# First unit's feed forward in float32 from weights right behind their bit operations, in a clustered attention with feed forward on one core

## The chip, the cores and the metric

The kernel runs on one core of one Trainium2 chip. The metric is the device time of one execution in microseconds (us). Before the change it is 861.57 us, the median of three runs (861.48 to 862.57).

## The reference

The reference is a clustered attention (4 batches, 8 heads, 768 positions, 64 numbers per head, 16 clusters per head) and a feed forward on its output. Every query and key is assigned to the nearest of its head's 16 centroids; a query attends only to keys of its own cluster.

```python
q_assign = np.argmax(np.einsum('bhsd,hcd->bhsc', q_n, c_n), axis=-1)
k_assign = np.argmax(np.einsum('bhsd,hcd->bhsc', k_n, c_n), axis=-1)
scores = np.where(q_assign == k_assign, scale * q @ k.T, -1e9)   # per batch and head
attn = softmax(scores)
x = (attn @ v) as 3072 tokens x 512
h = x @ w_in                                        # 512 x 2048
g = np.where(h >= 1, h, np.where(h <= -1, 0.0, (h + 1) ** 2 / 4))
out = (g @ w_out).astype(np.float32)                # 2048 x 512
```

The weights `w_in` and `w_out` reach the chip as float64; `q`, `k`, `v` are float32.

## The kernel before, in words

**Units and tiles.** The work is cut into 12 units, each a batch and a third of its queries (256 queries). A unit has four head pairs; each head pair has four attention tiles of 128 queries by 768 keys (`at_scores`, `at_soft`), and one product of probabilities and values with the row sums (`at_av`), which gives a quarter of the unit's `x`. A tile costs TensorE (PE) two to four matmuls into `pair`, VectorE (DVE) one custom operation that masks and takes the maximum (`sS<-pair,zero,er`), ScalarE (ACT) the exponential (`sS<-sS,sbi`), ACT a float16 copy (`hl<-sS`), GpSimd (POOL) the float16 rest (`hl<-sS,hl`), and the queue of SyncE (SP) a transposing DMA (`pT<-hl`). In unit 0 alone the tile stays float32 and PE transposes it (`pair<-idf,sS`); ACT copies it out (`pT<-pair`).

**Feed forward of a unit.** When the unit's `x` is there, it goes through 8 slices f of 256 hidden columns. `ffn1(u, f)` is 24 float16 matmuls 128x256: each operand is a sum of a float16 high and low half, and three of the four products are taken. Then DVE clamps (`r` from the bank), ACT squares, DVE multiplies and takes the maximum, ACT casts the high half of `g`, POOL subtracts for the low half. `ffn2(u, f)` is 12 float16 matmuls 128x512 that add into `pair`. `ffn_scale` makes a unit's powers of two and the clamps' bounds from the largest value of `x`'s source and of the weights, in short DVE operations.

**Weights.** 16 pieces (8 slices, `w_in` and `w_out`) arrive as float64 in `w`, `word` or two ends of other tiles. `w_bits` makes float32 of a piece: an ACT copy of the high words (`wk<-w`), a DVE shift (`wk<-wk`), PE sums of magnitudes (`<-wk,ones`) for a bound, and two DVE operations, which write in place (`w<-w,wk`, then `w<-w`; for the pieces in `word`, `word<-word,wk`, then `word<-word`). `w_sum` closes each slice's bound in short DVE operations (`w_am`, `w_iw`, `w_sw`). `w_split` then makes the float16 halves: an ACT scaling in place (`w<-w,w_sw`), an ACT cast (`w<-w`), a POOL subtraction (`w<-w`).

**What sets the order.** A recorder notes every operation with a step (`at(step, ...)`), plans all with rounds of forward and backward list scheduling from a table of costs (`BASE` rounds), then jiggles the priorities with a stored list of seeds (`NUDGES`), and issues each engine's instructions in the planned order, which is fixed at run time. Since one line issues all, every instruction of the profile of before stands at L351; groups are told apart by their names. A tile name's trailing number is its buffer. The steps around the change are `wat[i]` (bits of piece i), `sf` (feed forward), `PRO + 1` and `-7` (`v_bound` and `batch_scale` of batch 0, ahead of the first tile).

**Rings.** Temporary tiles rotate in rings: `wk` (two buffers), `word`, `r`, `g`, `x`. A tile can be written again once all that read it are done.

Of the kernel before, what the change touches and what calls it, by code (L numbers as in the profile page):

```python
# [474 lines left out]
def tile_clustered_attention_moe(  # L475
# [393 lines left out]
    def ffn_scale(us, fs):  # L869
# [4 lines left out]
        if n == GF:  # L874
            iw1, iw2, cs1 = (x[f0 // GF][:, :, a] for x, a in ((w_iw, 0), (w_iw, 1), (w_am, 0)))
        else:
            if not W:
                for i, (x, a) in enumerate(((w_iw, 0), (w_iw, 1), (w_am, 0))):
                    W[i] = const.tile([P, NF], F32, name=f"w_all{i}")
                    for g in range(NF // GF):  # L880
                        rec.gpsimd.tensor_copy(W[i][:, g * GF : (g + 1) * GF], x[g][:, :, a])
            iw1, iw2, cs1 = (W[i] for i in range(3))
# [129 lines left out]
    def at_av(b, hp, c):  # L1012
# [38 lines left out]
        xn = rs  # L1051
        if whole(b, c):
            rec.vector.scalar_tensor_tensor(
                out=xn, in0=pv, scalar=BX[b]["sv1"], in1=rs, op0=ALU.mult, op1=ALU.mult
            )
        else:
            rec.vector.tensor_tensor(out=xn, in0=pv, in1=rs, op=ALU.mult)
        if hp == 0:
            X[u] = new("x", [2, NP, CQ], F16)
        rec.scalar.copy(X[u][:, 0, hp], xn)  # L1060
        rec.gpsimd.tensor_tensor(out=X[u][:, 1, hp], in0=xn, in1=X[u][:, 0, hp], op=ALU.subtract)
# [285 lines left out]
```

## Time and profile before

| what | before |
|---|---|
| median of 3 runs | 861.57 us (861.48 to 862.57) |
| profiled execution, its own time | 860.33 us |
| span in its trace | 858.6 us |
| PE busy | 800.6 us (93%) |
| ACT busy | 664.1 us (77%) |
| DVE busy | 651.5 us (76%) |
| POOL busy | 546.6 us (64%) |
| DMA, mean rate over the span | 166 GB/s |

The trace is one execution. Its span runs from the first to the last recorded instruction; 1.73 us of the execution's time lie around it. "Busy" is the time in which at least one instruction of an engine was in flight. PE is the tensor engine's matmuls, PEld its loads of the stationary operand, which may lie beside matmuls. PEclk is the granted clock of the tensor engine as a share of full speed. A line of the timeline gives the start, the duration, the engine, the operation with the names of its tiles, and in brackets how long the engine had been idle and what released it. A float32 matmul appears in the trace as two records, a float16 one as one.

### The profile page before, as it was taken

The page shows a single profiled execution, that of the slowest core. Times are in us where ns is not written, and L with a number is a line of the kernel's source. Part 1 is how long each engine was busy: PE and PEld are TensorE (multiplying, and loading weights), DVE is VectorE, ACT ScalarE, POOL GpSimd, SP SyncE. Part 2 cuts the span into 40 slices and gives each one's busy share as a digit, 9 for nine tenths or more (in the row PEclk, how much of TensorE's full clock was granted, in tenths as well). Part 3 has the DMA queues.
Part 4 walks back from the last instruction along what each step waited for, and adds up shares of the span by engine and source line. Part 5 has one row for each costly group of instructions (what it writes and reads, how often), then busy time and mean ns, then how long its engine had stood idle before and what let it go on. Part 6 is the DMA issues. An engine that isn't in the chain of part 4 may idle for free.

```text
span 858.6 us, 19071 instructions
## 1 busy us (share of the span) xinstructions
PE 800.6 (93%) x7148; PEld 551.7 (64%) x7148; DVE 651.5 (76%) x1461; ACT 664.1 (77%) x1176; POOL 546.6 (64%) x527
## 2 busy tenths in 40 slices
PE   3666679999999999999999999999999999999998
PEld 3444456666676766767675766767676666676665
DVE  7999999988896877678887777668887767544322
ACT  6799999998777888778787788787788687776232
POOL 1146879887667777657666668757766667766222
PEclk9889989999999999999999999999999999999999
DMA  9896779789999989999999799999998778766100
GB/s 320 237 238 143 227 177 216 146 167 190 180 191 196 158 143 186 189 155 190 173 213 145 161 162 193 176 189 186 184 188 152 141 159 136 121 127 108 24 25 26
DMA packets 404766, 142.53 MB, mean 166 GB/s; under 512 B 372800, under 2 KB 396352, under 8 KB 404672
## 3 DMA queue, kind: packets, MB, share of 16 engines
q1 hardware_dynamic: 404672, 141.30, 82.1%
q8 instruction: 56, 0.92, 0.4%
q14 instruction: 38, 0.31, 0.1%
HBM read 40.40 MB, written 6.29 MB: 54 GB/s over the span
## 4 chain that ended last, share of the span: by engine, by line
PE 74%; DVE 15%; ACT 5%; issue 3%; DMA 2%; SPq 0%; POOL 0%; DVEq 0%; ACTq 0%
PE pair L351 37%; PE banka L351 10%; PE banki L351 9%; PE bankj L351 9%; PE bankh L351 9%; DVE sS L351 3%; DVE w L351 2%; ACT w L351 1%; ACT sS L351 1%; DMA kv<-in_k_dram 1%; DVE bankh L351 1%; DVE qn L351 1%; DVE r L351 1%; DVE wk L351 1%; DMA q<-qn 1%
## 5 line engine op out<-in xcount | busy, mean ns | idle before, releaser
L351 POOL TENSOR_TENSOR hl<-sS,hl 128x768 f16<-128x768 f32 x176 | 295.8, 1686 | 127.6 <-ACT hl L351 103.3
L351 PE MATMUL pair<-w,g 128*128 128x512 f16 x1152 | 271.2, 379 | 0.0
L351 PEld LDWEIGHTS <-w 128*128 128x128 f16 x2304 | 224.0, 98 | 48.3 <-issue 5.0
L351 DVE CUSTOM_DVE_ANT_0 sS<-pair,zero,er 128x768 f32<-128x768 f32 x192 | 193.9, 1011 | 50.9 <-PE pair L351 41.3
L351 ACT ACTIVATE sS<-sS,sbi 128x768 f32<-128x768 f32 x192 | 179.3, 934 | 60.0 <-DVE sbi L351 56.2
L351 PEld LDWEIGHTS <-g 128*128 128x128 f16 x1152 | 110.7, 98 | 114.3 <-issue 0.8
L351 PE MATMUL pair<-kv,q 128*128 128x384 f16 x768 | 159.9, 332 | 20.3 <-DVE sbi L351 8.7
L351 ACT CAST hl<-sS 128x768 f16<-128x768 f32 x176 | 143.7, 825 | 12.4 <-DMA pT<-hl 11.1
L351 POOL TENSOR_TENSOR g<-r,g 128x512 f16<-128x512 f32 x88 | 106.3, 1208 | 67.7 <-ACT g L351 56.1
L351 PEld LDWEIGHTS <-q 128*128 128x128 f16 x992 | 78.9, 99 | 76.9 <-issue 28.1
L351 PE MATMUL banka<-pT,kv 128*64 128x256 f16 (+1 forms) x1680 | 105.1, 279 | 0.2 <-DMA pT<-hl 0.2
L351 ACT ACTIVATE r<-r,f_ra,f_rs 128x512 f32<-128x512 f32 x88 | 71.3, 810 | 39.6 <-DVE r L351 39.4
L351 PEld LDWEIGHTS <-kv 128*64 128x64 f16 (+1 forms) x1824 | 92.7, 109 | 4.1 <-DMA kv<-n 0.9
L351 ACT CAST g<-r 128x512 f16<-128x512 f32 x88 | 53.7, 610 | 13.9 <-DVE r L351 9.4
L351 POOL TENSOR_TENSOR qn<-qn,phi 128x256 f16<-128x256 f16 x48 | 33.4, 715 | 30.9 <-DVE phi L351 21.4
L351 PE MATMUL bankh<-x,w 128*128 128x256 f16 x432 | 52.1, 273 | 0.7 <-DVE er L351 0.6
L351 PE MATMUL bankj<-x,w 128*128 128x256 f16 x408 | 50.1, 277 | 0.1
L351 POOL TENSOR_TENSOR w<-w 128x1024 f16<-128x1024 f32 x12 | 28.7, 2398 | 15.1 <-ACT w L351 15.0
L351 PE MATMUL banki<-x,w 128*128 128x256 f16 x312 | 37.6, 272 | 0.5 <-DVE r L351 0.5
L351 PE MATMUL banki<-wk,w 128*128 128x256 f16 x312 | 37.0, 272 | 0.0
L351 ACT ACTIVATE q<-q,phi 128x512 f16<-128x512 f16 x48 | 33.4, 715 | 4.3 <-DVE phi L351 2.7
L351 ACT ACTIVATION_READ_ACCUMULATOR sS<-sS,sbi 128x1 f32 x192 | 36.2, 189 | 0.0
(253 smaller groups left out, 1078.3 us busy)
## 6 DMA issues: line engine op xcount, KB each, us to landing
w<-in_moe_w_out_dram SPq DMA_DIRECT2D x14, 512.0 KB, 5.2
q<-in_q_dram SPq DMA_DIRECT2D x12, 512.0 KB, 4.9
kv<-in_k_dram SPq DMA_DIRECT2D x16, 384.0 KB, 4.2
kv<-in_v_dram SPq DMA_DIRECT2D x16, 384.0 KB, 4.2
out_dram<-o SPq DMA_DIRECT2D x11, 512.0 KB, 3.3
w<-in_moe_w_in_dram SPq DMA_DIRECT2D x10, 512.0 KB, 5.9
word<-in_moe_w_in_dram SPq DMA_DIRECT2D x6, 512.0 KB, 4.6
o<-in_v_dram SPq DMA_DIRECT2D x8, 384.0 KB, 4.1
```

Source lines behind the costliest of these rows:

```text
L351: fn(*args, **kw)
```

## The change

Unit 0's feed forward runs in float32. The last bit operation of a piece writes its float32 weights to `w32[a][f]`, the place in `wb` where the float16 halves later stand, and unit 0's matmuls read them there: 8 matmuls 128x256 for `ffn1` of a slice in place of 24, 4 matmuls 128x512 for `ffn2` in place of 12. Unit 0 has no `ffn_scale`, no cast and no subtraction for `g` and `x`; its `X[0]` is float32, written by DVE straight from the bank, and its clamp constants are fixed numbers. `w_split` comes later, after the slice's use by unit 0, and goes through a ring `ws` of three buffers (`wk[0]` and the two halves of `word`) back into `wb`. The bounds of the weights are closed by fours: `w_bound(g)`, two calls, each on 128x8, in place of one on 128x2 for each slice. The ring `w32` of the bit operations now has two buffers (`wk[0]` and `o`). `v_bound` and `batch_scale` of batch 0 stand at steps `VB + hp` and `VB + 5` in place of `PRO + 1` and -7. `WR`, the step from one piece's bits to the next, goes from 2.2 to 2.6; `BASE` from 40 to 29; `NUDGES` is another list with 147 entries in place of 201.

```diff
-BASE = 40
+BASE = 29
-    1600000002, 1600000012, 1600000016, 1600000020, 1600000031, 1600000035, 1600000041, 1600000076,
+    1700000013, 1700000016, 1700000028, 1700000032, 1700000035, 1700000049, 1700000073, 1700000096,
...
-    WA, WR = -4, 2.2
+    VB = 4
+    WA, WR = -4, 2.6
...
-    rings["w32"], rings["x"] = Ring(wk[:1]), Ring(tiles("x", 3, 4096) + wk + [word[:, :1024], word[:, 1024:]])
+    rings["w32"], rings["x"] = Ring(wk[:1] + rings["o"].bufs), Ring(tiles("x", 3, 4096) + wk + [word[:, :1024], word[:, 1024:]])
...
+        if hp == 0:
+            X[u] = new("x", [NP, CQ], F32) if u == 0 else new("x", [2, NP, CQ], F16)
         if whole(b, c):
             rec.vector.scalar_tensor_tensor(
-                out=xn, in0=pv, scalar=BX[b]["sv1"], in1=rs, op0=ALU.mult, op1=ALU.mult
+                out=X[u][:, hp], in0=pv, scalar=1 / UNIT, in1=rs, op0=ALU.mult, op1=ALU.mult
             )
+            return
...
+    w32 = [[wb[:, (2 * f + a) * 1024 : (2 * f + a + 1) * 1024] for f in range(NF)] for a in range(2)]
...
+    rings["ws"] = Ring([wk[0], word[:, :1024], word[:, 1024:]])
...
+        rec.vector.scalar_tensor_tensor(
+            out=dst, in0=hi, scalar=0x80000000, in1=to, op0=ALU.bitwise_and, op1=ALU.bitwise_or
+        )
...
+    def w_bound(g):
+        am, iw, sw = (x[:, g * GF : (g + 1) * GF].rearrange("p f a -> p (f a)") for x in (w_am, w_iw, w_sw))
+        mx = misc(2 * GF)
         rec.vector.tensor_scalar(
             out=mx, in0=am, scalar1=W_TINY, scalar2=2.0**-13 + 2.0**-19, op0=ALU.max, op1=ALU.mult
         )
         tiny_and(iw, mx, EXP_MASK2)
-        sw = new("w_sw", [2], F32, 4)
         rec.vector.reciprocal(sw, iw)
...
     def w_split(a, f):
-        t, tf = WL.pop((a, f))
-        tf = tf.bitcast(F32)
+        tf = new("ws", [1024], F32)
...
-        rec.scalar.activation(out=tf, in_=tf, func=AF.Copy, scale=sw)
+        rec.scalar.activation(out=tf, in_=w32[a][f].bitcast(F32), func=AF.Copy, scale=w_sw[:, f, a : a + 1])
...
+                for hp in range(NP if u == 0 else 0):
+                    rec.tensor.matmul(
+                        ph[:, s],
+                        w32[0][f].bitcast(F32)[:, hp * 256 + s * P : hp * 256 + (s + 1) * P],
+                        x[:, hp],
+                        start=(hp == 0),
+                        stop=(hp == NP - 1),
+                    )
...
+        if u == 0:
+            F[u, f] = r
+            return
...
-            at((b - 1) * SB + 22 + hp * 3 if b else PRO + 1, v_bound, b, hp)
-        at(b * SB - 13 if b else -7, batch_scale, b)
+            at((b - 1) * SB + 22 + hp * 3 if b else VB + hp, v_bound, b, hp)
+        at(b * SB - 13 if b else VB + 5, batch_scale, b)
...
+                if u == 0:
+                    sf = max(sf, wat[2 * f + 1] + 2)
+                    FS[u, f] = dict(io=1.0, lo=-1.0, hi=1.0, ra=half, rs=0.5, gs=1.0, first=f == 0, last=f == NF - 1)
+                    for x in range(2):
+                        at(max(sf + 3.5, wat[-1] + 1), w_split, x, f)
...
-        if a:
-            for x in range(2):
-                at(wat[i], w_split, x, f)
+        if a and f % GF == GF - 1:
+            at(wat[i] + 0.5, w_bound, f // GF)
```

The order on ACT, before, among unit 0's last tiles (`sS<-sS,sbi` is a tile's exponential, `pT<-pair` the copy of its transpose): the scaling `w<-w,w_sw` and the cast `w<-w` are a split.

```order
82 L351 ACTIVATE w_78<-w_78,w_sw_152 128x1024
83 L351 ACTIVATE sS_86,rs_163<-sS_86,sbi_156 128x768
84 L351 ACTIVATE sS_87,rs_163<-sS_87,sbi_157 128x768
85 L351 CAST w_78<-w_78 128x1024
86 L351 ACTIVATE pT_164<-pair_79 128x6x128
87 L351 CAST x_72<-rb_170 128x256
88 L351 ACTIVATE pT_164<-pair_80 128x6x128
89 L351 ACTIVATE q_66<-q_66,phi_149 128x512
90 L351 ACTIVATE wk_69<-w_78 128x1024
```

The order on ACT now, around the first split of the whole program, among tiles that follow unit 0's; `wk_69<-word_71` opens the bits of the last piece that arrives in `word`, `g_75<-g_75,half` is unit 0's square.

```order
129 L345 ACTIVATE wk_69<-word_71 128x1024
130 L345 ACTIVATE sS_85,rs_151<-sS_85,sbi_145 128x768
131 L345 CAST hl_167<-sS_86 128x768
132 L345 ACTIVATE g_75<-g_75,half 128x512
133 L345 ACTIVATE q_65<-q_65,phi_142 128x512
134 L345 CAST hl_168<-sS_87 128x768
135 L345 ACTIVATE wk_69<-w_78,w_sw 128x1024
136 L345 CAST w_78<-wk_69 128x1024
137 L345 ACTIVATE sS_86,rs_151<-sS_86,sbi_146 128x768
```

All 16 splits stand behind row 134 now; before, 12 of the 16 scalings stood ahead of row 134, the first of them at row 28.

The order on DVE, before, up to the fourth product of unit 0 (`rb<-banka,sv,rb`, the last quarter of its `x`):

```order
242 L351 RECIPROCAL f_hi_179<-f_inv_174 128x4
243 L351 RECIPROCAL f_lo_184<-banki 128x4
244 L351 TENSOR_SCALAR banki<-banki 128x4
245 L351 TENSOR_TENSOR f_gs_204<-banki,f_inv_174 128x4
246 L351 SCALAR_TENSOR_TENSOR w_78<-w_78 128x1024
247 L351 TENSOR_SCALAR f_ra_194<-banki 128x4
248 L351 SCALAR_TENSOR_TENSOR f_rs_199<-banki,f_inv_174 128x4
249 L351 SCALAR_TENSOR_TENSOR rb_170<-banka,sv_144,rb_170 128x256
```

The same place now; `x_72<-banka,rb_160` is the same product's last quarter.

```order
200 L345 SCALAR_TENSOR_TENSOR w_78<-word_71 128x1024
201 L345 ISA sS_85,sbi_145<-pair_80,zero,er_140 128x768
202 L345 ISA sbi_145 128x1
203 L345 TENSOR_REDUCE aq_125<-q_65 128x4
204 L345 RECIPROCAL w_sw<-w_iw 128x8
205 L345 TENSOR_REDUCE w_am<-bankh 128x2
206 L345 SCALAR_TENSOR_TENSOR x_72<-banka,rb_160 128x256
```

43 rows fewer stand ahead of this product: the short operations of `ffn_scale` and of the bounds, and some of the weights' bits.

More of the change, by code (lines that the diff above doesn't have):

```diff
@@ L655, in batch_scale @@
         e.update(isx=isx, sv=sv)
-        if b == 0:
-            e["sv1"] = const.tile([P, 1], F32, name="sv1")
-            rec.vector.tensor_scalar(out=e["sv1"], in0=sv, scalar1=1 / UNIT, scalar2=None, op0=ALU.mult)
     def transpose(out, nat, ps=None):
@@ L873, in ffn_scale @@
         f0, n = fs[0], len(fs)
[L874 to L882, printed above, removed]
+        iw1, iw2, cs1 = w_iw[:, :, 0], w_iw[:, :, 1], w_am[:, :, 0]
         def small(tag, cols=n):
@@ L1050, in at_av @@
         rec.scalar.copy(rs, rb)
-        xn = rs
+        if hp == 0:
+            X[u] = new("x", [NP, CQ], F32) if u == 0 else new("x", [2, NP, CQ], F16)
         if whole(b, c):
             rec.vector.scalar_tensor_tensor(
-                out=xn, in0=pv, scalar=BX[b]["sv1"], in1=rs, op0=ALU.mult, op1=ALU.mult
+                out=X[u][:, hp], in0=pv, scalar=1 / UNIT, in1=rs, op0=ALU.mult, op1=ALU.mult
             )
[L1056 to L1061, printed above, removed]
+            return
+        rec.vector.tensor_tensor(out=rs, in0=pv, in1=rs, op=ALU.mult)
+        rec.scalar.copy(X[u][:, 0, hp], rs)
+        rec.gpsimd.tensor_tensor(out=X[u][:, 1, hp], in0=rs, in1=X[u][:, 0, hp], op=ALU.subtract)
     X = {}
@@ L1067, in tile_clustered_attention_moe @@
     WL, WS = {}, {}
+    w32 = [[wb[:, (2 * f + a) * 1024 : (2 * f + a + 1) * 1024] for f in range(NF)] for a in range(2)]
     w1 = [view(wb[:, 2 * f * 1024 : (2 * f + 1) * 1024], [2, DM // P, 256], F16) for f in range(NF)]
     w2 = [view(wb[:, (2 * f + 1) * 1024 : (2 * f + 2) * 1024], [2, 2, DM], F16) for f in range(NF)]
-    w_am, w_iw = ([const.tile([P, GF, 2], F32, name=f"{x}{g}") for g in range(NF // GF)] for x in ("w_am", "w_iw"))
+    w_am, w_iw, w_sw = (const.tile([P, NF, 2], F32, name=x) for x in ("w_am", "w_iw", "w_sw"))
+    half = const.tile([P, 1], F32, name="half")
+    nc.gpsimd.memset(half, 0.5)
     WP = {}
     wd = 2 if w_wide else 1
+    rings["ws"] = Ring([wk[0], word[:, :1024], word[:, 1024:]])
     def w_load(a, f, part=None):
@@ L1102, in w_bits @@
         t = WL[a, f][0][:, (part or 0) * 512 :][:, :n]
+        dst = w32[a][f][:, (part or 0) * 512 :][:, :n]
         tf = t.bitcast(F32)
@@ L1106, in w_bits @@
             w_sum(a, f, part)
[L1107 to L1110 removed]
+            rec.vector.tensor_copy(dst, raw)
             return
@@ L1149, in w_sum @@
             return
-        am, iw = (x[f // GF][:, f % GF] for x in (w_am, w_iw))
-        mx = pc[:, 2, :2]
-        rec.vector.tensor_reduce(out=am, in_=pc[:, :2], op=ALU.max, axis=AX.X)
+        rec.vector.tensor_reduce(out=w_am[:, f], in_=pc[:, :2], op=ALU.max, axis=AX.X)
+    def w_bound(g):
+        am, iw, sw = (x[:, g * GF : (g + 1) * GF].rearrange("p f a -> p (f a)") for x in (w_am, w_iw, w_sw))
+        mx = misc(2 * GF)
         rec.vector.tensor_scalar(
@@ L1180, in ffn1 @@
             with rec.group():
-                for hp in range(NP):
+                for hp in range(NP if u == 0 else 0):
[6 more added lines that the diff above has]
+                    )
+                for hp in range(0 if u == 0 else NP):
                     for i, (wa, xa) in enumerate(((0, 0), (0, 1), (1, 0))):
@@ L1190, in ffn1 @@
         phf = ph.rearrange("p s q -> p (s q)")
-        r = new("hl" if u == NU - 1 else "r", [2 * CQ], F32, 1)
+        r = new("g" if u == 0 else "hl" if u == NU - 1 else "r", [2 * CQ], F32, 1)
         rec.vector.tensor_scalar(out=r, in0=phf, scalar1=e["lo"], scalar2=e["hi"], op0=ALU.max, op1=ALU.min)
@@ L1209, in ffn2 @@
         po = F[u]
+        if u == 0:
+            with rec.group():
+                for s in range(2):
+                    for t in range(CT):
+                        rec.tensor.matmul(
+                            po[t],
+                            g[:, s * CQ + t * P : s * CQ + (t + 1) * P],
+                            w32[1][f].bitcast(F32)[:, s * DM : (s + 1) * DM],
+                            start=(f == 0 and s == 0),
+                            stop=(f == NF - 1 and s == 1),
+                        )
         terms = [(s, i, *x) for s in range(2) for i, x in enumerate(((0, 0), (0, 1), (1, 0)))]
@@ L1213, in ffn2 @@
         parts = [(terms, [t]) for t in range(CT)] if end else [(terms[:3], range(CT)), (terms[3:], range(CT))]
-        for part, ts in parts:
+        for part, ts in parts if u else ():
             with rec.group():
@@ L1303, in tile_clustered_attention_moe @@
             at(wat[i], w_bits, a, f, p)
-        if a:
-            for x in range(2):
-                at(wat[i], w_split, x, f)
+        if a and f % GF == GF - 1:
+            at(wat[i] + 0.5, w_bound, f // GF)
     rec.step = -99
```

25 lines of the change are left out of this document (4 added, 21 removed), and 44 rows, old and new, of the table NUDGES.

## The prediction

> **What bounds the kernel now.** I read the page's slices first, then busy time by stage, then the chain of events around the first feed forward. In the slices each digit is a fortieth of the span:
>
> ```profile
> span 858.6 us, 19071 instructions
> PE 800.6 (93%) x7148; PEld 551.7 (64%) x7148; DVE 651.5 (76%) x1461; ACT 664.1 (77%) x1176; POOL 546.6 (64%) x527
> PE   3666679999999999999999999999999999999998
> ```
>
> PE has nines from about the sixth slice to the end and is loose only before. The windows put numbers on that (columns: stretch, its length, then PE, PEld, DVE, ACT, POOL busy, granted clock, DMA share, GB/s):
>
> ```profile
> 0.00:111.00 111.00, 65.98 (x643) 45.40 (x644) 104.01 (x255) 95.86 (x148) 49.05 (x66) 0.92 0.83 232
> 111.00:236.70 125.70, 119.57 (x1072) 82.14 (x1071) 112.54 (x257) 112.59 (x201) 100.29 (x85) 0.99 0.89 179
> 236.70:400.00 163.30, 163.17 (x1498) 113.94 (x1495) 129.85 (x284) 129.10 (x242) 113.60 (x110) 1.00 0.97 177
> 400.00:800.00 400.00, 397.39 (x3553) 274.33 (x3552) 288.07 (x644) 309.36 (x563) 271.48 (x257) 1.00 0.86 161
> ```
>
> Up to 111 us PE is idle for 45 us while DVE is busy for 104 of 111: DVE paces the start. From 111 to 236.7 PE idles 6.1 us; after it 2.7 us in 563. So a change ahead of 236.7 passes to the end one for one if PE's remaining work stays the same, and what happens there must be followed to one event. I take unit 1's last `ffn1` (M), since it needs the last weights' halves:
>
> ```profile
> 233.77 2.75 PE L351 MATMUL pair<-w,g 128*128 128x512 f16 x12
> 236.36 0.46 PE L351 MATMUL bankh<-cT,kv 128*128 128x32 f16 x12
> 236.66 2.78 PE L351 MATMUL bankj<-x,w 128*128 128x256 f16 x24
> 239.28 0.81 PE L351 MATMUL pair<-kv,q 128*128 128x384 f16 x4
> ```
>
> M is at 236.66. Start to next start also gives two prices: 24 float16 matmuls 128x256 take 2.62 us (109 ns each), 12 of 128x512 take 2.59 us (216 ns). The first feed forward starts so:
>
> ```profile
> 105.74 2.59 DVE L351 SCALAR_TENSOR_TENSOR w<-w 128x1024 uint32<-128x1024 uint32 x1
> 108.40 0.47 DVE L351 SCALAR_TENSOR_TENSOR rb<-banka,sv,rb 128x256 f32<-128x256 f32 x1
> 109.48 0.40 ACT L351 CAST x<-rb 128x256 f16<-128x256 f32 x1
> 109.95 0.98 POOL L351 TENSOR_TENSOR x<-rb,x 128x256 f16<-128x256 f32 x1 [2.70 <-ACT x L351]
> 110.98 3.04 POOL L351 TENSOR_TENSOR w<-w 128x1024 f16<-128x1024 f32 x1
> 111.09 1.27 PE L351 MATMUL bankj<-x,w 128*128 128x256 f16 x5
> ```
>
> DVE comes to the last quarter of `x` at 108.40, then ACT and POOL add 2.2 us before PE starts at 111.09.
>
> **The first feed forward starts earlier.** The order puts 43 fewer DVE rows ahead of that product: four bit operations, two shifts, one tile, one maximum of V, and some 30 short rows. The rows that price them (instructions by form between 18 and 109 us, then two of the timeline):
>
> ```profile
> L351 DVE SCALAR_TENSOR_TENSOR w<-w 128x1024 uint32<-128x1024 uint32 x10 | 14.1, 1412 | 0.0
> L351 DVE SCALAR_TENSOR_TENSOR w<-w,wk 128x1024 uint32<-128x1024 uint32 x11 | 13.4, 1220 | 0.0
> L351 DVE TENSOR_SCALAR wk<-wk 128x1024 uint32<-128x1024 uint32 x12 | 9.1, 759 | 0.5 <-ACT wk L351 0.5
> 109.72 0.68 DVE L351 TENSOR_SCALAR wk<-wk 128x1024 uint32<-128x1024 uint32 x1
> 11.49 2.67 DVE L351 TENSOR_REDUCE v_am<-kv 128x1 bf16<-128x768 f32 x3
> 14.08 0.41 DVE L351 TENSOR_REDUCE mx<-bankh 128x16 f32<-128x256 f32 x1
> ```
>
> Successive DVE instructions overlap by about 0.08 us, so 4×1.15 + 2×0.61 + 0.93 (a tile) + 0.85 (a maximum) + some 30 short ones at 0.13 = 11.6 us less. Next, the bit operations run slower where POOL subtracts: `w<-w` took 1.41 on average and 2.59 at 105.74, the shift 0.76 against 0.68. With no split ahead, 10×0.19 + 12×0.08 and the longest single excess go, about 4.5 us together (bounds 2 to 5.5). Against it, `v_bound` leaves the start, where its 2.67 us stood in DVE's wait for the first labels (the maximum at 14.08): DVE now idles there, 2.5 us (bounds 0 to 2.7). So the last quarter ends at 108.87 − 11.6 − 4.5 + 2.5 = 95.3, and with no cast or subtraction behind it PE starts at about 95.5, 15.6 us earlier. ACT and PE can follow: ACT loses 12 splits from that stretch.
>
> **Unit 0's matmuls cost more.** No matmul of this shape in float32 is in the trace; the nearest is unit 0's product with V, against its float16 form:
>
> ```profile
> 56.65 2.76 PE L351 MATMUL banka<-pT,kv 128*64 128x256 f32 x24
> 240.27 2.13 PE L351 MATMUL banka<-pT,kv 128*64 128x256 f16 x36
> L351 PEld LDWEIGHTS pair<-idf,sS 128*128 128x128 f32 x96 | 11.8, 156 | 13.6 <-ACT sS L351 13.2 <-issue 0.4
> L351 PEld LDWEIGHTS <-w 128*128 128x128 f16 x277 | 27.5, 100 | 6.8 <-issue 1.0
> ```
>
> The 24 float32 records are 12 matmuls, in pairs: 460 ns a pair against 118, so 3.9 times, and I take 4. A slice costs 8×4×0.109 + 4×4×0.216 = 6.95 us in place of 5.21: 1.74×8 = 13.9 us more on PE. The load of float32 weights took 156 ns against 100. I take it as hidden, since the float32 product with V stayed at the rate of its passes; bounds 0 to 11 us (rival below). The Trainium skill, "TensorE: Matmul & The Clock Gate", section "Weight-path perf modes — Fast Weight Load (FWL) and DoubleRow", says that the fast load is on for 128 weights whose type is not FP32, which speaks against the change; the two rows agree in direction, and by it nothing is lost while a load is shorter than the matmul ahead of it.
>
> **PE alone.** From PE's start to M, before has 114.3 us of PE work in 125.6 us. To it come the 13.9 us; 2.9 us of tiles that used to stand ahead of the start; and 1.6 us that now stands ahead of M instead of behind it: 132.7 us. With 6 to 11 us of idle time and half clock (before lost 11.3), M by PE alone would be 95.5 + 132.7 + 6 to 11 = 234.2 to 239.2, at best guess 235.5.
>
> **The splits stand later, and ACT must do them all.** This is the step on which I choose. The ring of the splits starts with `wk[0]`, which is free when DVE has done the first bit operation of the third piece staged in `word`:
>
> ```profile
> 145.50 1.52 DVE L351 SCALAR_TENSOR_TENSOR word<-word,wk 128x1024 uint32<-128x1024 uint32 x1
> ```
>
> In before it ends at 147.02. DVE's work ahead of it is about the same in the order of after (0.4 us more), so it comes at 147.0 − 5.5 (POOL's hindrance up to there) + 2.5 + 0.4 = 144.4 (bounds 142 to 147). The order then has 127 ACT instructions from the first split's scaling to the cast of slice 7's `w_in`. Their prices (ACT by form, 60 to 170 us):
>
> ```profile
> L351 ACT ACTIVATE sS<-sS,sbi 128x768 f32<-128x768 f32 x26 | 24.4, 940 | 1.5 <-DVE sbi L351 1.3
> L351 ACT CAST hl<-sS 128x768 f16<-128x768 f32 x16 | 13.0, 824 | 0.0
> L351 ACT CAST w<-w 128x1024 f16<-128x1024 f32 x9 | 10.3, 1147 | 0.0
> L351 ACT ACTIVATE w<-w,w_sw 128x1024 f32<-128x1024 f32 x8 | 10.1, 1257 | 1.7 <-DVE w L351 1.7
> L351 ACT ACTIVATE r<-r,f_ra,f_rs 128x512 f32<-128x512 f32 x7 | 5.7, 808 | 0.0
> L351 ACT CAST g<-r 128x512 f16<-128x512 f32 x6 | 3.7, 611 | 1.3 <-DVE rs L351 1.3
> L351 ACT ACTIVATE qn<-q,sq 128x256 f16<-128x256 f32 x8 | 3.8, 514 | 0.0
> ```
>
> Neighbours overlap by about 0.1 us, except that an exponential's read of its sum follows it (0.93 in all). 21 exponentials are 19.5, 22 casts `hl` 16.1, 15 scalings 17.1, 15 casts of weights 15.5, 10 squares 7.2, 7 casts `g` 3.6, together 79.0; 37 shorter ones at 0.41 (the `qn` row) are 15. So ACT needs 94 us without a gap, and POOL's subtraction follows:
>
> ```profile
> L351 POOL TENSOR_TENSOR w<-w 128x1024 f16<-128x1024 f32 x12 | 28.7, 2398 | 15.1 <-ACT w L351 15.0
> ```
>
> M = 144.4 + 94 + 2.4 = 240.8, 5.3 us behind PE alone and 4.1 us later than before. ACT was busy for 112.6 of 125.7 us in that window of before; now it has slack ahead of 144 and none behind. After M, PE has 1.6 us less to do. The bounds of M are 142 + 92 + 2.4 = 236.4 and 147 + 95 + 2.4 + 1.6 (PE's tiles and ACT waiting for each other) = 246.
>
> **Small edits.** The bounds by fours and the fixed constants are in the DVE count; they save POOL four copies. Behind M the order differs through the new list. The last stretch:
>
> ```profile
> 800.00:858.60 58.60, 54.48 (x392) 35.89 (x390) 17.00 (x23) 17.20 (x26) 12.21 (x11) 0.99 0.05 19
> ```
>
> PE idles 2.7 us from M to 800 and 4.1 here, so I price the new list at nothing, bounds −2 to +2.
>
> **The sum.** Against the profiled execution (858.6 + 1.73 = 860.33) the change is +4.1 − 1.6 = +2.5. The median lies 1.24 us higher, so 861.57 + 2.5 = 864.1, rounded to 864.0. Its own range, with the bounds of M, is 859.7 to 869.3, the ends only if every bound falls to one side.
>
> **The rivals.**
>
> *PE alone sets M* (faster). If the splits keep ahead of unit 1, because DVE frees `wk[0]` earlier or ACT runs denser, M is 235.5 and the time 861.57 − 1.1 − 1.6 = 858.9. For it: PE was the engine without idle time from 111 us on. Against it: the last 94 us of ACT work begin only at 144. It decides if the first split starts before about 139.
>
> *Both nearly meet* (no difference). The splits come a little earlier or denser, or the start comes at 98 in place of 95.5: M at about 238, time 861.3. This also covers the case that the change does not do what it says, the first feed forward held back by another wait than DVE's.
>
> *POOL sets M* (slower). From the first split to slice 7's subtraction POOL has 22 subtractions `hl`, 15 of weights, 7 of `g`, 6 of `x` and 15 short ones:
>
> ```profile
> L351 POOL TENSOR_TENSOR hl<-sS,hl 128x768 f16<-128x768 f32 x34 | 58.0, 1711 | 13.9 <-ACT hl L351 12.4 <-DVE sbi L351 1.1
> L351 POOL TENSOR_TENSOR g<-r,g 128x512 f16<-128x512 f32 x14 | 17.4, 1243 | 10.8 <-ACT g L351 10.8
> L351 POOL TENSOR_TENSOR x<-rb,x 128x256 f16<-128x256 f32 x11 | 8.6, 783 | 2.7 <-ACT x L351 2.7
> ```
>
> That is 37.6 + 36.0 + 8.7 + 4.7 + 8 = 95 us, from 146.6 (the first cast's end): 241.6, level with ACT. The means hold some stretched rows already. If half the subtractions of weights take the 3.04 us of the one at 110.98, beside DVE, that is 7.5×0.64 = 4.8 more, M = 246.4, and the time 861.57 + 9.7 − 1.6 = 869.7. The Trainium skill, "SBUF — State Buffer", states that DVE and GpSimd lock a shared port pair and that the loser blocks for a whole instruction; the 2.59 us at 105.74 agrees, and by it the splits' move shifts that loss from the start to the stretch before M.
>
> *Float32 loads in the open* (slower). 8×12 = 96 matmuls, two records each: 192×(156 − 100) = 10.8 us on PE's path: M = 246.3, so 869.6. Against it: the float32 rows above.
>
> **How the numbers follow.** About 0.2%, 1.72 us, is what a measurement of this kernel can tell from no change: faster is below 859.85, slower above 863.29. The forecast (ACT) has 0.39, of which 0.05 falls within 0.2%; PE alone 0.25; both nearly meeting 0.23; POOL 0.08; loads 0.05. So faster 0.25, same 0.28, slower 0.39 − 0.05 + 0.08 + 0.05 = 0.47. The range takes PE alone's lower end (234.2: 857.6) as 857.5 and goes up to 869.0, nearly the forecast's upper end; POOL's case, the loads and the tails are left out.
>
> **What would show it.** Right: the first `ffn1` at 94 to 98 with float32 records; the first split's scaling on ACT at 142 to 147; ACT without a gap from there; M at 240 to 242, with PE's idle time between 200 and 240 ended by POOL `w` or ACT `w`. Wrong: PE without gaps before M and M at 235 (PE alone); POOL dense and ACT waiting for it (POOL); float32 `ffn1` of 8 matmuls over 4.2 us (loads); a first `ffn1` after 100, which undoes the first term.

## The result, and the profile after

The changed kernel takes 855.91 us (median of 6 runs, 855.04 to 856.83), the kernel before 862.0 us beside it (6 runs, 859.35 to 862.72). The ratio is 0.9934, with a 95% interval of 0.992 to 0.9949: faster by 0.66%, where 864.0 was forecast. The time lies below the range. The profiled span went from 858.6 to 854.1 us.

The page of the changed kernel, busy time and PE's slices (each a fortieth of the span):

```profile
span 854.1 us, 18789 instructions
PE 808.4 (95%) x7052; PEld 557.1 (65%) x7052; DVE 641.5 (75%) x1408; ACT 653.2 (76%) x1158; POOL 530.1 (62%) x510
PE   3676999998999999999999999999999999999997
```

PE's nines begin at the fifth slice instead of the seventh. The windows, cut at the first feed forward (91.9), the first split (141.4) and M, unit 1's eighth first product (234.66):

```profile
0.00:91.90 91.90, 60.50 (x619) 42.28 (x620) 83.41 (x209) 69.00 (x115) 18.77 (x47) 0.93 0.89 256
141.40:234.66 93.26, 88.01 (x738) 59.71 (x736) 80.08 (x171) 89.88 (x148) 87.98 (x62) 1.00 0.87 172
234.66:400.00 165.34, 162.99 (x1462) 112.70 (x1459) 125.86 (x285) 132.71 (x248) 118.89 (x113) 1.00 0.90 171
400.00:800.00 400.00, 400.00 (x3603) 277.03 (x3601) 288.70 (x643) 310.17 (x566) 267.64 (x259) 1.00 0.85 159
```

Ahead of the first feed forward POOL is busy for 18.8 us in place of 49.1, ACT for 69.0 in place of 95.9. That work now stands between 141 and 235 us, where ACT (89.9 of 93.3) and POOL (88.0) are nearly full. The first feed forward, on DVE and then PE:

```profile
91.64 0.41 DVE L345 SCALAR_TENSOR_TENSOR x<-banka,rb 128x256 f32<-128x256 f32 x1
91.91 1.89 PE L345 MATMUL banki<-x,w 128*128 128x256 f32 x8
94.29 1.89 PE L345 MATMUL banki<-x,w 128*128 128x256 f32 x8
96.02 1.89 PE L345 MATMUL bankh<-x,w 128*128 128x256 f32 x8
```

The last quarter of `x` ends at 92.05, against 108.87, and PE starts 19.2 us earlier than before (it may take the first three head pairs while the last quarter is made). M, with PE's rows around it:

```profile
232.28 2.13 PE L345 MATMUL banka<-pT,kv 128*64 128x256 f16 x36
234.34 0.47 PE L345 MATMUL bankh<-cT,kv 128*128 128x32 f16 x12
234.66 2.78 PE L345 MATMUL bankj<-x,w 128*128 128x256 f16 x24
```

M came 2.0 us earlier (236.66 before), and from M to the end it takes 619.4 us in place of 621.9. Together that is the span's 4.5 us. Up to M, PE has some 10 us more work (185.5 us before, 195.7 now, by its windows) and waits 12 us less.

### The profile page after: what moved, and what is told of

Its sections match the earlier page's. It is cut to its first block, busy times and chain, and to the rows that moved or that the text cites. A ratio compares the mean times of both kernels' runs of the same rounds, so it can differ in the third digit from the quotient of the medians.

```text
span 854.1 us, 18789 instructions
## 1 busy us (share of the span) xinstructions
PE 808.4 (95%) x7052; PEld 557.1 (65%) x7052; DVE 641.5 (75%) x1408; ACT 653.2 (76%) x1158; POOL 530.1 (62%) x510
## 4 chain that ended last, share of the span: by engine, by line
PE 69%; DVE 1%; ACT 0%; issue 0%; DVEq 0%
PE pair L345 34%; PE banka L345 10%; PE bankh L345 9%; PE banki L345 9%; PE bankj L345 7%; DVE sS L345 0%; DVE bankh L345 0%; ACT hl L345 0%; DVE qn L345 0%; ACT qn L345 0%; DVE n L345 0%; ACT r L345 0%; DVE mx L345 0%; DVE o L345 0%; ACT o L345 0%
## 5 line engine op out<-in xcount | busy, mean ns | idle before, releaser
L345 PE MATMUL pair<-w,g 128*128 128x512 f16 (+1 forms) x1120 | 277.0, 391 | 0.5 <-ACT o L345 0.5
L345 PEld LDWEIGHTS <-w 128*128 128x128 f16 x2112 | 204.6, 98 | 43.8 <-issue 5.6
L345 PEld LDWEIGHTS <-g 128*128 128x128 f16 x1056 | 101.0, 98 | 106.1 <-issue 1.9
L345 POOL TENSOR_TENSOR g<-r,g 128x512 f16<-128x512 f32 x80 | 94.0, 1176 | 56.8 <-ACT g L345 53.9
L345 ACT ACTIVATE r<-r,f_ra,f_rs 128x512 f32<-128x512 f32 x80 | 64.7, 809 | 31.7 <-DVE r L345 31.5
L345 PE MATMUL bankj<-x,w 128*128 128x256 f16 (+1 forms) x424 | 58.2, 289 | 4.3 <-DVE r L345 1.6
L345 ACT CAST g<-r 128x512 f16<-128x512 f32 x80 | 48.9, 611 | 14.4 <-DVE r L345 8.5
L345 PE MATMUL bankh<-x,w 128*128 128x256 f16 (+1 forms) x376 | 46.5, 277 | 0.0
L345 PE MATMUL banki<-x,w 128*128 128x256 f16 (+1 forms) x288 | 40.5, 291 | 0.4 <-DVE w_iw L345 0.4
L345 POOL CAST rr<-rs 128x4 f16<-128x4 f32 x48 | 15.8, 328 | 36.6 <-DVE bankj L345 21.0
```

The costliest lines, as they stand in the source:

```text
L345: fn(*args, **kw)
```

## The experiments

All edits but the two of the list keep the planned order of the kernel that they start from: the planner sees the unchanged costs, and the edit is made when the instructions are issued. vb_early and split2_early then move the few operations that they name. A table first; "start" is PE's first matmul of the feed forward (in late4 it takes three head pairs at 93.1 and has the last quarter of `x` only after 97.2), "split" the first split's scaling, all from the one profiled execution of each. "Ratio" is to the kernel before, run beside it, with its interval.

| kernel | edit | us | ratio | start | split | M |
|---|---|---|---|---|---|---|
| before | – | 862.0 | 1 | 111.1 | – | 236.7 |
| after | – | 855.91 | 0.9934 (0.992–0.9949) | 91.9 | 141.4 | 234.7 |
| before_list0 | no list of seeds | 870.29 | 1.0107 (1.0092–1.0122) | 114.5 | – | 242.3 |
| after_list0 | no list of seeds | 857.5 | 0.9963 (0.995–0.9976) | 92.4 | 140.0 | 236.6 |
| cast2 | after, 16 split casts twice | 867.59 | 1.0077 (1.0061–1.0092) | 93.2 | 142.4 | 246.6 |
| cast2_six | after, 6 split casts twice | 860.22 | 0.999 (0.9981–0.9999) | 91.3 | 140.9 | 238.5 |
| scale_less | after, 6 scalings short | 854.57 | 0.993 (0.9908–0.9951) | 91.9 | 141.2 | 233.4 |
| ffn1_half | after, 13.9 us less PE, unit 0 | 856.46 | 0.9953 (0.9939–0.9967) | 93.2 | 140.8 | 234.0 |
| u1_cut | after, 10.7 us less PE, unit 1 | 854.87 | 0.9928 (0.9902–0.9953) | 93.2 | 142.4 | 234.6 |
| both_less | scale_less and u1_cut | 856.06 | 0.9943 (0.9925–0.9961) | 91.9 | 141.5 | 235.9 |
| late4 | after, 4.5 us more DVE at 91 us | 861.2 | 1.0 (0.999–1.001) | 93.1 | 146.6 | 239.8 |
| dve_less | after, 4.6 us less DVE | 855.59 | 0.9936 (0.9921–0.9951) | 92.0 | 141.0 | 234.2 |
| vb_early | after, V's maxima early | 855.53 | 0.9938 (0.9923–0.9953) | 93.6 | 142.4 | 235.6 |
| relu_u0 | after, clamp from DVE to ACT | 857.69 | 0.9957 (0.9941–0.9974) | 92.5 | 143.6 | 236.4 |
| split2_early | after, two splits early | 856.14 | 0.9945 (0.993–0.996) | 93.3 | – | 235.4 |
| before_pool2 | before, split subtractions twice | 892.62 | 1.0367 (1.0349–1.0384) | 127.5 | – | 266.4 |
| before_memset | before, memset for subtraction | 862.6 | 1.0026 (1.0014–1.0039) | 110.8 | – | 238.8 |
| before_scale | before, scalings short | 863.97 | 1.0021 (1.0011–1.0032) | 114.1 | – | 241.2 |
| before_scale_memset | both | 862.82 | 1.0021 (1.0008–1.0035) | 111.3 | – | 239.3 |

Kernels that are the same up to 90 us start their feed forward at 91.3 to 93.3 us (the last section shows that the granted clock goes with this), so a difference of one or two microseconds between single profiles is no finding; the medians and the distance from the split to M carry the argument.

**Is it the list?**

```diff
-NUDGES = (
-    1700000013, 1700000016, 1700000028, 1700000032, 1700000035, 1700000049, 1700000073, 1700000096,
...
+NUDGES = ()
```

> The changed kernel with an empty list of seeds, so that only the planner's rounds set the order. Theory (the float32 feed forward makes the gain, by an early start of unit 0's feed forward on PE): the first feed forward still starts near 92 us, against 111 in the kernel before, and the time stays below that of the kernel before without its list by 3 to 9 us; by itself it is 857 to 866. Rival (the new list makes the gain): the two kernels without lists take the same time within 2 us, both above 862.

> The kernel before with an empty list of seeds. Theory: 863 to 870, with the first feed forward at 109 to 114 us, and 3 to 9 us above the changed kernel without its list. Rival (the list makes the gain): within 2 us of the changed kernel without its list.

The rival falls. Without lists the change is worth more: 0.9963 / 1.0107 = 0.986, about 12 us. The old list takes 9 us off the kernel before, the new one some 2.5 us off the changed one (0.9963 against 0.9934). Each kernel kept its own number of planner's rounds, 40 and 29. The early start is there without a list, the first matmuls of the feed forward in after_list0 and in before_list0:

```profile
92.44 1.89 PE L324 MATMUL banki<-x,w 128*128 128x256 f32 x8
```

```profile
114.46 1.91 PE L324 MATMUL bankj<-x,w 128*128 128x256 f16 x8
```

**Does ACT set M, or PE?** First more work on ACT:

```diff
         rec.scalar.copy(whi, tf)
+        rec.nodes[-1].times = 2
...
-                for fn, args, kw in x.calls:
-                    fn(*args, **kw)
+                for i, (fn, args, kw) in enumerate(x.calls * x.times):
+                    if i not in x.drop:
+                        fn(*args, **kw)
```

> The changed kernel in its own order, with each split's ACT cast issued twice: 16 casts of 1.04 us more on ACT, 14 of them (14.6 us) up to slice 7's w_in half. Theory (PE alone sets M, the halves are ready 6.5 us before): slice 7's w_in subtraction ends at 228.2 + 14.6 = 242.8, M waits for it, 234.7 + 8.1 = 242.8, and the time is 855.9 + 8.1 = 864. Rival (ACT already sets the end): 855.9 + 14.6 = 870.5. Rival (ACT is nowhere near): 856.

> The changed kernel in its own order, with the ACT cast of the splits of slices 1, 2 and 3 issued twice: 6 x 1.04 = 6.2 us more on ACT ahead of M. New theory (ACT sets the pace, 3.4 us idle): M and the time 3 to 6 us later, 859 to 862. Rival (PE sets M and the halves are 6.5 us early): 856.

From the split to M it took 93.3 us in the changed kernel, 104.2 in cast2 and 97.6 in cast2_six: 10.9 us for 14.6 us of casts, 4.3 for 6.2. This does not fit the theory that PE alone sets M until the halves come (864, 856): extra ACT work costs about 0.7 us for each microsecond from the first on. Then less work on PE, in unit 0 and in unit 1:

```diff
                         stop=(hp == NP - 1),
                     )
+                    rec.open.drop = (1, 2)
```

> The changed kernel in its own order, leaving out two of four head pairs in unit 0's first product: 32 float32 matmuls 128x256 fewer, 32 x 0.433 = 13.9 us of PE work. Theory (PE work sets M until the halves do, 6.5 us on): M goes to 228.3 and the time to 855.9 - 6.4 = 849.5. Rival (only PE's work counts): 855.9 - 13.9 = 842.0. Rival (the splits already set M): no change, 856.

```diff
+                    rec.open.drop = (1, 2, 4, 5, 7, 8, 10) if u == 1 else ()
                     for i, (wa, xa) in enumerate(((0, 0), (0, 1), (1, 0))):
```

> The changed kernel in its own order, leaving out 14 of 24 matmuls in each slice of unit 1's first product: 1.53 us a slice, 10.7 us of PE work less between 170 and M. New theory (from the first split at 141 to M, ACT sets the pace with at most 3.4 us of idle time, PE waits on it through the tiles): M comes 1 to 3 us earlier, the time is 853 to 855. Rival (PE's work sets M): M comes 6.5 us earlier, when the halves are ready, and the time is 849.4 or less.

ffn1_half settles what the float32 work of unit 0's first product costs. Its windows up to the end of unit 0's last `ffn1` and from there to M (unit 0's last three `ffn2`, in float32 too, lie in the second), then the same two of the changed kernel:

```profile
93.20:160.00 66.80, 54.44 (x368) 34.76 (x367) 63.52 (x109) 54.91 (x94) 46.97 (x35) 1.00 0.93 193
160.00:234.00 74.00, 68.30 (x610) 45.45 (x610) 63.43 (x144) 71.26 (x118) 68.75 (x50) 1.00 0.89 173
```

```profile
91.90:161.50 69.60, 66.85 (x432) 46.87 (x431) 65.95 (x112) 56.00 (x95) 46.16 (x35) 1.00 0.88 188
161.50:234.66 73.16, 68.32 (x611) 45.45 (x610) 62.54 (x142) 70.39 (x117) 67.88 (x50) 1.00 0.87 173
```

PE has 12.4 us less to do in the first stretch, and the split and M stand where they stood: PE just waits longer (12.4 us idle in place of 2.8), and the time is not shorter. Unit 0's extra passes lie beside work of DVE. In u1_cut nearly the same holds behind 161 us: 9.2 us less PE work shortens the stretch by 1.1 us. What PE saves there it mostly waits for DVE's `sbi`, that is for a tile's scores to be read out of `pair`: 7.8 us in 8 waits, against 1.3 in 2 in the changed kernel (window, then PE's row of waits in u1_cut and in the changed kernel):

```profile
162.50:234.60 72.10, 59.11 (x513) 35.83 (x513) 64.44 (x142) 70.28 (x117) 67.93 (x50) 1.00 0.91 177
```

```profile
PE pair L346 <- DVE sbi L346: 7.8, 8, 1.9
```

```profile
PE pair L345 <- DVE sbi L345: 1.3, 2, 0.9
```

Then less work on ACT, and on both:

```diff
+        if f in (4, 5, 6):
+            rec.nodes[-1].calls[0][2].update(out=tf[:, :64], in_=w32[a][f].bitcast(F32)[:, :64])
```

> The changed kernel in its own order, with the ACT scaling of the splits of slices 4, 5 and 6 on 64 of 1024 columns (the rest of these halves is left out): 6 x 1.05 = 6.3 us less ACT work between unit 0's end and M. Theory (ACT, busy for 70.4 of 73.2 us there, sets that stretch, with POOL and PE 5 us behind): M 3 to 5 us earlier, the time 851 to 853. Rival (PE sets it): 856.

> The edit of scale_less and that of u1_cut together (14 of 24 matmuls of unit 1's first product left out): ACT 6.3 and PE 10.7 us less before M. Theory (three engines are within 5 us of each other there, and POOL is left with 67.9 of 73.2 us): M 4 to 6 us earlier, 850 to 852, hardly more than by scale_less alone. Rival (PE and ACT limit in turns): 846 to 849.

```profile
161.20:233.40 72.20, 68.16 (x612) 45.46 (x611) 61.90 (x142) 66.64 (x118) 68.18 (x50) 1.00 0.86 175
```

```profile
161.50:235.90 74.40, 60.45 (x512) 36.30 (x511) 65.88 (x143) 66.53 (x118) 66.94 (x50) 0.98 0.89 171
```

Here the theory that ACT alone sets the stretch falls too. With 3.8 us less ACT work (first line, scale_less) it is 1.0 us shorter, and with PE and ACT both relieved (second line, both_less) it is not shorter at all. This profile is the slowest of both_less's five executions, but its median, 856.06, is no shorter either. So work added on ACT between the first split and M costs most of its length, while work taken from ACT, from PE or from both behind 161 us gives 1 us or nothing. PE, ACT and POOL are each busy for 68 to 70 of 73 us there, DVE for 62.5, and a tile goes from PE through DVE, ACT, POOL and a DMA back to PE; what holds the stretch once two of them are relieved stays open.

**Does DVE set the start and unit 0's feed forward?**

```diff
             apply_absolute_value=True,
         )
+        rec.nodes[-1].times = 5 if u == 2 else 1
```

> The changed kernel in its own order, with the maximum over Q of unit 2 (DVE, 1.13 us start to start), which stands just ahead of the last quarter of unit 0's x, issued five times: 4.5 us of DVE work more at 90 us. New theory (DVE's bit operations on the weights pace unit 0's feed forward from its start to about 158 us, and 14 us of float32 work are hidden in PE's waiting there): everything on DVE comes 4.5 us later, unit 0's last float32 matmul at 166, the first split at 146, M at 239, the time 860.4. Rival (PE's work from its start on sets M, as the prediction's rival had it, less the 7.6 us of idle time): 856 to 858.

```diff
             out=dst, in0=hi, scalar=0x80000000, in1=to, op0=ALU.bitwise_and, op1=ALU.bitwise_or
         )
+        if f < 2:
+            rec.nodes[-1].gone = True
+            rec.nodes[-2].calls[0][2]["out"] = dst
```

> The changed kernel in its own order, leaving out the last bit operation (the sign) of the four pieces of slices 0 and 1: 4 x 1.14 = 4.6 us less DVE work ahead of the first feed forward. Theory (DVE's work paces the start and up to 141 us, one for one): start at 87 to 89, the first split at 137, the time 851.5. Rival (other waits lie close behind DVE at the start, as with V's maxima moved): 854 to 856.

Again one direction only. In late4 the five maxima take 6.23 us at 90.69, the last quarter of `x` follows at 97.23, the split at 146.6, and the time is 861.2, 5.3 us more:

```profile
90.69 6.23 DVE L346 TENSOR_REDUCE aq<-q 128x4 bf16<-128x1024 f32 x5
96.83 0.19 DVE L346 RECIPROCAL w_sw<-w_iw 128x8 f32<-128x8 f32 x1
96.94 0.37 DVE L346 TENSOR_REDUCE w_am<-bankh 128x2 f32<-128x256 f32 x1
97.23 0.41 DVE L346 SCALAR_TENSOR_TENSOR x<-banka,rb 128x256 f32<-128x256 f32 x1
```

In dve_less 4.6 us less DVE work leaves the start at 92.0. (The granted clock from 60 to 92 us was 0.89 there and 1.00 in the changed kernel; by the last section that may hide about a microsecond.) DVE waits for PE instead, 2.0 us for tiles (`sS`) and 4.3 us ahead of maxima (`mx`), against 0.4 and 2.4 in the changed kernel. DVE's waits up to 93 us, dve_less and then the changed kernel (in all, times, longest):

```profile
DVE mx L345 <- PE bankj L345: 3.0, 2, 2.4
...
DVE sS L345 <- PE pair L345: 2.0, 4, 0.7
DVE mx L345 <- PE bankh L345: 1.3, 1, 1.3
```

```profile
DVE mx L345 <- PE bankj L345: 2.4, 1, 2.4
...
DVE sS L345 <- PE pair L345: 0.4, 1, 0.4
```

Two more edits in this direction were meant to be faster than the changed kernel:

```diff
+        early("v load", "weights")
+        early("v bound", "labels")
```

> The changed kernel with V's loads of batch 0 issued ahead of the weights' first loads and three maxima of V (0.87 us each) put into DVE's 2.4 us wait for the first labels, all else in its own order. Theory (DVE paces): DVE is about 2.2 us earlier from there on, and the time is 853.7. Rival (no DVE time at the start reaches the end, or the weights' loads come later by as much): 855.9.

```diff
+            clamp, square, top = (x.calls for x in rec.nodes[-3:])
+            relu = dict(out=r, in_=phf, func=AF.Relu, bias=half, scale=0.5)
+            square[:] = [(nc.scalar.activation, (), relu), (nc.scalar.activation, (), dict(out=r, in_=r, func=AF.Square))]
+            top[0][2].update(in0=r, scalar=1.0, in1=phf, op0=ALU.min)
+            clamp.clear()
```

> The changed kernel in its own order, with unit 0's clamp taken from DVE: ACT makes max(h/2 + 1/2, 0) from the bank and squares it, and DVE's one operation takes min(., 1) and the maximum with h. DVE has 8 x 0.6 = 4.9 us less and ACT as much more up to unit 0's end. Theory (DVE's work, busy for 65.9 of 69.6 us, paces unit 0's feed forward, and ACT has 13 us of idle time there): unit 0's end and the first split 2 to 4 us earlier, the time 852 to 854. Rival (other waits lie close behind, as when DVE had less work at the start): 855 to 857.

vb_early filled DVE's wait and gained nothing: the three maxima begin only at 12.29, behind V's DMA, and DVE later waits for PE's tiles. Its timeline, and its row of waits:

```profile
12.29 2.67 DVE L354 TENSOR_REDUCE v_am<-kv 128x1 bf16<-128x768 f32 x3 [0.62 <-DMA kv<-in_v_dram]
```

```profile
DVE sS L354 <- PE pair L354: 2.2, 2, 1.5
```

relu_u0 gave the work to ACT, in the stretch where ACT has 13 us of idle time, and is not faster (0.9957 against 0.9934, intervals that just overlap); unit 0's eight first products took 71.7 us in place of 69.6. Moving splits the other way, ahead of 141 us, did not help either:

```diff
+SOON = {(0, 0): (105, 118), (0, 1): (121, 123)}
```

> The changed kernel in its own order, except that the splits of w_in's slices 0 and 1 are made in halves (through r, which unit 0 does not use) in ACT's waits between 105 and 125 us: 4.4 us less ACT work and 4.3 us less POOL work between 141 and M. Theory (from the first split to M ACT sets the pace, and PE has 5.2 us of idle time there): M 2 to 4 us earlier, the time 852 to 854. Rival (PE sets M): 856. Rival (POOL's subtractions then hinder DVE's bit operations, which pace that stretch): 857 to 859.

It took 856.14. (Each split's second half reads columns that the first half's rest has overwritten, so the data differ.) The same with four splits (split4_early) took 859.58 us (ratio 0.9982, 0.9972 to 0.9992), M at 238.1, where 851 to 853 was expected. That is the time of its rival of hindered bit operations (858 to 861), but not its reason: between 92 and 160 us four bit operations `w<-w` took 1.34 us on average, against 1.86 in the changed kernel. From 111.0 to 141.4 us in split2_early (first line) POOL is busy for 5.9 us more than in the changed kernel (second line) and PE for 1.5 us less:

```profile
111.00:141.40 30.40, 27.99 (x204) 18.46 (x203) 28.66 (x51) 24.14 (x43) 21.99 (x18) 1.00 0.86 181
```

```profile
111.00:141.40 30.40, 29.51 (x218) 19.82 (x217) 29.91 (x53) 22.55 (x39) 16.06 (x16) 1.00 0.87 190
```

**Why does the first feed forward start 19 us earlier?** Four edits of the kernel before, on the splits that stand ahead of it there:

```diff
         rec.gpsimd.tensor_tensor(out=wlo, in0=tf, in1=whi, op=ALU.subtract)
+        rec.nodes[-1].times = 2
```

> The kernel before in its own order, with each split's POOL subtraction issued twice: 9 more of 2.1 to 2.4 us each up to 100 us, where POOL is busy for 49 of 111 us. Theory (a POOL subtraction beside DVE's two-input bit operations holds DVE up, which cost the kernel before about 7 us up to the fourth product): the fourth product and the first feed forward come 3 to 7 us later, the time is 864 to 869. Rival (POOL does not hinder DVE): the first feed forward stays within 1 us of 111, the time 861 to 863.

```diff
         rec.gpsimd.tensor_tensor(out=wlo, in0=tf, in1=whi, op=ALU.subtract)
+        rec.nodes[-1].calls = [(nc.gpsimd.memset, (wlo, 0.0), {})]
```

> The kernel before in its own order, with each split's POOL subtraction replaced by a memset of the low halves (so the low halves of the weights are left out): POOL writes as much but reads nothing. Theory (what POOL reads beside DVE's two-input operations holds DVE up, about 7 us up to the fourth product): the first feed forward at 103 to 106 in place of 111, the time 854 to 858. Rival (the splits' place ahead of the first feed forward costs only ACT's and POOL's own time): the first feed forward stays at 109 to 111.

> The kernel before in its own order, with the ACT scaling of every split on 64 of 1024 columns (the rest of the weights' halves is left unscaled): some 1.15 us less ACT work for each of the 10 splits ahead of 100 us. Theory (ACT, busy for 40.0 of 40 us from 60 to 100, paces the start, and the splits are a quarter of its work there): the first feed forward at 103 to 107 in place of 111, the time 854 to 858. Rival (DVE alone, busy for 38.9 of 40, paces it): the first feed forward at 110 to 111, the time 860 to 862.

> The edits of before_scale and before_memset together (ACT's scaling short, POOL's subtraction a memset, so both halves of the weights are incomplete). Theory (ACT and DVE are tied at the start, each alone gives little): the first feed forward at 98 to 104, the time 850 to 857, clearly earlier than by either alone. Rival (what is left, the count of DVE's instructions ahead, holds it): within 1.5 us of before_scale.

Doubling POOL's subtractions moved the start by 16.4 us, far more than expected; DVE, with the same instructions, was busy for 116.5 us up to there in place of 104.0. The windows of before_pool2:

```profile
0.00:111.00 111.00, 69.63 (x587) 47.73 (x588) 100.94 (x226) 86.15 (x130) 60.16 (x66) 0.81 0.71 207
111.00:127.50 16.50, 9.29 (x58) 4.64 (x56) 15.52 (x29) 10.99 (x19) 13.61 (x11) 0.71 0.68 169
```

Taking their reading away moved it by 0.3 us, and shortening ACT's scalings, alone or with it, did not move it forward at all. The windows of before_memset and of before_scale_memset:

```profile
0.00:111.00 111.00, 69.94 (x645) 48.25 (x646) 101.35 (x255) 96.62 (x148) 33.23 (x66) 0.90 0.81 232
```

```profile
60.00:100.00 40.00, 29.16 (x243) 20.09 (x244) 36.65 (x84) 34.60 (x61) 15.22 (x23) 0.84 0.66 166
```

DVE is busy for 2.7 us less up to 111 than in the kernel before (101.35 against 104.01), POOL for 16 us less, ACT for 5 us less from 60 to 100 in the second, and the product stays at 108. The freed time went into waits: from 20 us to the product DVE waits for 0.5 us in the kernel before and for 3.3 in before_memset, for PE, ACT and POOL. And the row of 2.59 us that the prediction put down to a split's subtraction is still there without one, beside POOL's subtractions for tiles:

```profile
105.51 2.50 DVE L351 SCALAR_TENSOR_TENSOR w<-w 128x1024 uint32<-128x1024 uint32 x1
```

```profile
102.08 4.85 POOL L351 TENSOR_TENSOR hl<-sS,hl 128x768 f16<-128x768 f32 x3 [4.54 <-ACT hl L351]
```

In the kernel before, too, POOL works on tiles at that moment and not on a split:

```profile
102.14 5.11 POOL L351 TENSOR_TENSOR hl<-sS,hl 128x768 f16<-128x768 f32 x3 [1.46 <-ACT hl L351]
```

The times agree: before_memset, before_scale and before_scale_memset are each 0.2 to 0.3% slower than the kernel before, and no interval reaches down to 1.

So more of the splits' work holds the start up, but less of it does not bring it forward while the order stays. By exclusion the order itself is left: what stands ahead on DVE (42 instructions less in the traces, 12.7 to 13.9 us by their rows, where the prediction counted 11.6), and `x`, whose cast and subtraction stood between DVE and PE (2.2 us). These make 15 to 16 of the 19.2 us. This is argued from the rows and not shown by a run; the rest was not tried apart, nor which part of the change (the later splits, the second buffer of `w32`, the later `v_bound`, the bounds by fours) lets the product stand earlier.

## Why the prediction was wrong

**The step that failed** is the one on which the prediction said that it chose: "The order then has 127 ACT instructions from the first split's scaling to the cast of slice 7's `w_in`." The planned order names no slices in its rows. With each split's slice written beside it, slice 7's `w_in` is the fourteenth split, 111 instructions on; the fifteenth, which was counted to, is slice 6's `w_out`, for which M does not wait. The casts and subtractions of the fourteenth and the fifteenth:

```profile
224.60 1.05 ACT L345 CAST w<-word 128x1024 f16<-128x1024 f32 x1
236.13 1.05 ACT L345 CAST w<-word 128x1024 f16<-128x1024 f32 x1
```

```profile
226.06 2.13 POOL L345 TENSOR_TENSOR w<-word,w 128x1024 f16<-128x1024 f32 x1
238.56 2.13 POOL L345 TENSOR_TENSOR w<-word,w 128x1024 f16<-128x1024 f32 x1
```

The fifteenth's halves are there at 240.69, and the prediction's sum for it was 240.8: it started 3 us too late and took the run of instructions behind it as a little too short. The fourteenth's are there at 228.19, 6.5 us ahead of M. So M did not wait for the splits' halves at all; which engine holds the stretch ahead of it stays open, as said above. By the prediction's sum, less the 11.5 us that lie between the two casts in this trace, the right split would have come at 144.4 + 82.5 + 2.4 = 229.3, PE alone at 235.5 would have been the later, and the forecast would have been that rival's 858.9, faster.

**The rival "PE alone sets M"** came nearest in its number (M 235.5, measured 234.7) and has the sign right, but its reason does not hold: 12.4 or 9.2 us less PE work up to M left M where it was. The number was luck: a start that was forecast too late and work that is partly free made up for each other. The 114.3 us of PE work that this sum begins with stand in no row; its own window has 119.57 us busy in 125.70.

**The start.** 95.5 was forecast, 91.9 measured. Up to the last quarter of `x` DVE was busy for 101.9 us before and for 83.4 now. Of these 18.5 us the prediction had 11.6 by count and 4.5 as POOL's hindrance. (Its sum for the second counts the row of 2.59 us twice, since the mean of 1.41 holds it; without that it gives 2.9.) Form by form, the two traces give 13.9 us for the instructions that no longer stand there and 5.8 for instructions of the same form that took longer before, 1.2 more than the 18.5 because neighbours overlap. So both terms were there, and both too small. But the second is no gain by itself: in before_memset 3.8 of the 5.8 us are gone (2.7 of DVE's busy time), and the start stays. The wait that `v_bound` leaves open is there (2.4 us, before `mx` at 14.06; forecast 2.5), but filling it gained nothing.

**Float32 on PE.** Eight records, four matmuls, take 1.73 us from start to start (94.29 to 96.02), against 4×0.436 = 1.74 forecast: the price was right. The loads stayed hidden, though they are longer than the row that the prediction used:

```profile
L345 PEld LDWEIGHTS bankj<-x,w 128*128 128x128 f32 x64 | 11.9, 190 | 3.9 <-DVE w_am L345 2.3
L345 PEld LDWEIGHTS <-q 128*128 128x128 f16 x98 | 8.0, 97 | 9.4 <-issue 5.4
```

What was wrong is that it was put on the path: ffn1_half shows that half of the first product's 28 us is free. The rival of loads in the open fell.

**Split to M.** The first split came at 141.4, not 144.4 (bounds 142 to 147), because DVE's start was 3 us earlier. Behind it ACT was as full as forecast (89.9 of 93.3 us).

**POOL.** Its 95 us from the first cast to the fifteenth's subtraction (the split that was counted to) were 240.69 − 143.94 = 96.8 us. Stretched subtractions were the exception: 3.11 us once, 2.13 in most rows.

**Behind M** 1.6 us less was forecast, 2.5 measured. The list, priced at nothing, is worth 9 us to the kernel before and 2.5 to the changed one, so the comparison of two lists hides half of what the change itself brings. And the prediction put the median 1.24 us above the profiled execution, as in the kernel before; in the changed kernel it lies 0.03 above (855.91 and 855.88). M (−6.1), the rest behind it (−0.9) and this offset (−1.2) make up the 8.1 us between 864.0 and 855.9, but for rounding.

## What to carry to other kernels

Before summing a chain to "the instruction that needs it", make sure which instance it is: rows that print alike hide the slice, and one split's difference turned the sign here. In a kernel whose order a planner has balanced, a test that adds work and one that takes it away are both needed: adding 4.5 us to DVE or 6 us to ACT cost 4 to 5 us, while taking as much or more from DVE, ACT or PE gave 0 to 1.3 us. And extra passes on the busiest engine can be free where that engine waits for another: ask for its idle time in that stage, not for its share of the span.

## What the runs showed of the hardware

A float32 load of 128x128 took 190 ns here and 156 ns in the transposes of the kernel before, a float16 load 97. It stayed hidden behind records that follow each other every 216 ns, with little to spare. The rule of the Trainium skill that the prediction weighed ("TensorE: Matmul & The Clock Gate", "Weight-path perf modes — Fast Weight Load (FWL) and DoubleRow": no fast load for FP32) agrees with the two loads' rows; here it cost nothing.

The granted clock at the start differs between executions of kernels that are alike up to there. cast2, cast2_six, ffn1_half, u1_cut, scale_less, both_less and the changed kernel issue the same up to 92 us. From 60 to 92 us the clock was 0.84 in three of them (cast2, ffn1_half, u1_cut), and PE's feed forward began at 93.2; it was 0.95 or 1.00 in the other four, where it began at 91.3 to 91.9. The changed kernel, then ffn1_half:

```profile
60.00:92.00 32.00, 24.82 (x268) 17.41 (x265) 31.78 (x72) 25.60 (x44) 7.05 (x9) 1.00 0.83 228
```

```profile
60.00:92.00 32.00, 26.93 (x258) 19.40 (x257) 30.31 (x68) 24.20 (x39) 5.94 (x9) 0.84 0.77 212
```

Where an edit took work from ACT or POOL in the kernel before, the clock from 60 to 100 us was 0.83 to 0.87 in place of 1.00, and PE was busy longer (29.2 us in before_scale_memset, above, against 27.3 in the kernel before):

```profile
60.00:100.00 40.00, 27.27 (x270) 18.33 (x268) 38.87 (x87) 40.00 (x62) 27.81 (x24) 1.00 0.67 185
```

That may be part of why these edits did not bring the start forward; it was not tried by itself. It hides no gain in the time: two executions of before_memset with a mean clock of 0.986 took 861.6 and 862.1 us, and four of the kernel before beside them, at 0.987 and 0.988, took 859.1 to 861.0.

POOL's subtraction of a split held up a short DVE operation in the kernel before: the operation took 2.01 us and ended at 48.54, right behind the subtraction (48.45). In before_memset the same operation took 0.23 us:

```profile
46.33 2.12 POOL L351 TENSOR_TENSOR w<-w 128x1024 f16<-128x1024 f32 x1 [3.91 <-ACT w L351]
46.53 2.01 DVE L351 TENSOR_TENSOR banki<-zs,has 128x64 f32<-128x64 f32 x1
```

```profile
46.19 0.23 DVE L351 TENSOR_TENSOR banki<-zs,has 128x64 f32<-128x64 f32 x1
```

By the Trainium skill, "SBUF — State Buffer", section "SBUF: two separate sides", only a GpSimd operation that reads SBUF holds up DVE's two-input operations. These rows agree, and so does DVE's mean for the second bit operation, which went from 1412 to 1343 ns with POOL's memsets, with the one stretched row beside POOL's tile subtractions left.
